# One graph and a list scheduler in place of hand-interleaved streams, with the spectral part reordered: block-sparse attention followed by a gated long convolution

## The chip, the cores and the metric

One core of a Trainium2 chip runs the whole kernel. The metric is device time in microseconds (us). The kernel before took 307.49 us (median of 3 runs, 306.24 to 308.87) when the prediction was made. Engine names are those of the profile: PE is TensorE (matmuls), PEld its weight loads, DVE is VectorE, ACT is ScalarE, POOL is GpSimd, SP the engine whose queue issues most DMAs.

## The reference

```python
# q, k, v: (4 batches, 8 heads, 768, 64) f32
k_rep = k.reshape(B, H, 12, 64, D).mean(axis=3)          # mean key of each block of 64
gate = einsum('bhsd,bhnd->bhsn', q, k_rep)               # causal; each query keeps its 3 best
                                                         # blocks and its own
attn = softmax(where(mask & causal, q @ k.T / 8, -1e9)) @ v
x = attn as (B, 768, 512)
x1, x2, x3 = split(x @ w_proj)                           # w_proj: 512 x 1536
x2c = irfft(rfft(x2, axis=1) * rfft(filter_fft, axis=0)) # circular convolution over 768
out = (x1 * x2c * x3) @ w_out
```

The DFT runs along the sequence and the projection along the features, so they commute: DFT(x) @ W2 = DFT(x @ W2). The change uses this.

## The kernel before

Work comes in 16 groups (a pair of heads in a batch). A group has a preparation (transposes of K and Q, the gate, the block mask), scores, exp, P@V and a normalisation. Four groups give a batch, on which the convolution part runs ("hyena" in the code). Scores are matmuls over 128 rows: 64 features, 12 rows that carry the block mask, 52 rows of zeros. All attention-phase results share 8 PSUM banks: 2 pairs for scores, 4 single ones for the rest.

Names in the lines below: `kn`, `qn`, `vn` are loaded K, Q and V; `kp`, `qp`, `xp` transposes; `kmb` (`km` after the change) the key sums of the blocks; `gn` the gate; `nm`, `mt`, `ms` the mask; `sp` the scores, `ex` their exp; `po` P@V; `xT` the transposed attention output, `xe` and `xo` (`eo` after) its even and odd sums; `x13p` and `prod` the projections x1 and x3 and their product; `Y` the filtered spectrum, `cv` its inverse transform, `yT` the gated product, `op` and `osb` the result. After the change every PSUM bank is called `ps`.

```python
    def score_piece(st, h, pi):                  # Kt, Qt: 128 rows, 76 of them used
        for (col, kc, q0, w) in PIECES[pi]:
            nc.tensor.matmul(sp[:, col:col + w], lhsT=kt[:, P * kc:P * (kc + 1)], rhs=qt[:, q0:q0 + w], ...)
        nc.scalar.activation(ex[:, 0:w], sp[:, 0:w], AF.Exp, scale=ESC)
    ...
    def pair_out(st, j):                         # per pair: transpose, even and odd sums
        ...
        nc.vector.tensor_copy(xT[:, j, :], xp[:, 0:S])
        eng.tensor_tensor(xe[:, j, :], xT[:, j, 0:HS], xT[:, j, HS:S], op=ALU.add)
        eng.tensor_tensor(xo[:, j, :], xT[:, j, 0:HS], xT[:, j, HS:S], op=ALU.subtract)
    ...
    def hyena_gen(st, last=False):               # per batch, after its four pairs
        for nm_, src in (("x2e", xe), ("x2o", xo)):
            for t in range(HC):
                for dc in range(DC):
                    nc.tensor.matmul(pp, lhsT=src[:, dc, P * t:P * (t + 1)], rhs=wp[:, dc, Dm:2 * Dm], ...)
                nc.scalar.copy(dst[:, t, :], pp)         # x2p -> x2e, x2o
                yield 0.85
        for c in range(HC):
            dft_fwd(x2[0], x2[1], c, 0, xa)              # then the DFT of the whole batch
            ...                                          # products t, spectrum Y, x13, cv, yT, op
```

The order comes from generators that each announce a guessed cost, merged by their progress; the framework's own scheduler may then still move instructions on all engines but SP.

```python
    def merge(streams):
        while True:
            live = [s_ for s_ in streams if s_.alive]
            if not live:
                return
            min(live, key=lambda s_: s_.key()).step()
    ...
            streams = [Stream(attn_gen(st), T_ATT), Stream(later_preps(b), NP * (T_PREP + 0.1))]
            ... streams.append(Stream(hyena_gen(prev), T_HY))      # the batch before
            merge(streams)
    ...
        with tc.manual_schedule(engines={mybir.EngineType.SP}):
            schedule()
```

The softmax here doesn't subtract the row's maximum and nothing guards it: scores larger than these inputs give would overflow.

## Time and profile before

| | before |
|---|---|
| median, us | 307.49 |
| span of the profiled run, us | 305.3 |
| PE / DVE / ACT / POOL busy, us | 254.0 / 218.7 / 176.3 / 138.0 |
| PE streaming (estimate, below), us | 216 |
| first score matmul (start), last P@V matmul (end), us from start | 18.0, 262.4 |

The page of the profiled run: busy time and share by engine, then the span in 40 equal slices (tenths busy), then the chain of work that ended last.

```profile
PE 254.0 (83%) x2309; PEld 153.9 (50%) x2309; DVE 218.7 (72%) x673; ACT 176.3 (58%) x277; POOL 138.0 (45%) x202
...
PE   3485897797999698987997798988996999899891
...
DMA  9998999699387308276759119094902000310005
...
PE 43%; DVE 31%; POOL 8%; ACT 6%; DMA 5%; issue 4%; SPq 1%; ACTq 0%; DVEq 0%
```

No engine is full, and the chain hops between PE and DVE. PE's busy time needs care: a 512-column matmul is logged with 0.38 us, but 24 of them in a row took 5.19 us in the traces, one per 0.216 us. In the same way I read 0.163 us at 384 columns (12 in 1.95 us) and 0.031 us for a P@V matmul of 65 (27 in 0.85 us). Counts times such spacings give the *PE streaming* used below, an estimate: 216 us for the whole program. (The Trainium skill, "Perfetto Trace Analysis", section "Identifying the Most-Contended Engine", says that matmul busy time is no good measure because matmuls are pipelined; the trace agrees: 254.0 us are logged where some 216 us stream.)

By stage: each row is a stretch of time, then its length, then busy us and instruction count of each engine, the granted clock, the DMA engines' share and GB/s.

```profile
core 0: us, PE busy (x) PEld busy (x) DVE busy (x) ACT busy (x) POOL busy (x), PEclk, DMA share, GB/s
0.00:79.00 79.00, 56.03 (x550) 36.96 (x551) 60.05 (x219) 52.00 (x75) 44.81 (x78) 0.98 0.97 184
79.00:145.00 66.00, 58.79 (x561) 35.91 (x560) 48.28 (x157) 37.38 (x62) 30.46 (x43) 0.95 0.55 115
145.00:211.00 66.00, 58.66 (x567) 35.91 (x565) 48.31 (x157) 39.94 (x65) 30.50 (x44) 0.97 0.57 123
211.00:262.00 51.00, 46.53 (x451) 28.55 (x449) 36.86 (x101) 31.51 (x49) 26.86 (x35) 0.97 0.24 52
262.00:305.30 43.30, 34.02 (x195) 16.57 (x191) 25.16 (x42) 15.49 (x30) 5.40 (x4) 0.98 0.19 73
```

### The profile page before, as it was taken

How to read it: one execution, taken by the hardware profiler on the slowest of the kernel's cores; microseconds unless marked ns; L12 is line 12 of the kernel's file. 1: busy time of each engine (PE TensorE's matmuls, PEld its weight loads, DVE VectorE, ACT ScalarE, POOL GpSimd, SP SyncE). 2: the span in 40 equal slices, each digit the busy share in tenths (PEclk: the TensorE clock that was granted, in tenths of full speed). 3: DMA queues.
4: the chain of work that ended last, by engine and by line, in shares of the span. 5: the costliest groups of instructions: out<-in, count | busy, mean ns of one | idle time of the engine just before them, and what ended most of it. 6: DMA issues, size and time to landing. Idle time of an engine off the chain costs nothing.

```text
span 305.3 us, 6432 instructions
## 1 busy us (share of the span) xinstructions
PE 254.0 (83%) x2309; PEld 153.9 (50%) x2309; DVE 218.7 (72%) x673; ACT 176.3 (58%) x277; POOL 138.0 (45%) x202
## 2 busy tenths in 40 slices
PE   3485897797999698987997798988996999899891
PEld 2332674464555366654654466544544566444430
DVE  7699985856589768665589768665599676339790
ACT  2349987584847435665856356656865467541314
POOL 7886226542339723532159453531188344205100
PEclk9999999997999789999999799999999899999999
DMA  9998999699387308276759119094902000310005
GB/s 169 215 261 198 140 210 179 144 173 201 72 152 139 73 1 164 50 150 201 179 104 184 29 34 178 5 268 151 196 19 50 4 6 3 139 67 2 0 0 206
DMA packets 87311, 36.00 MB, mean 118 GB/s; under 512 B 76936, under 2 KB 83440, under 8 KB 87280
## 3 DMA queue, kind: packets, MB, share of 16 engines
q1 hardware_dynamic: 85168, 33.50, 50.7%
q0 software_dynamic: 2112, 2.10, 4.7%
q8 instruction: 18, 0.29, 0.4%
q14 instruction: 13, 0.11, 0.1%
HBM read 24.64 MB, written 6.29 MB: 101 GB/s over the span
## 4 chain that ended last, share of the span: by engine, by line
PE 43%; DVE 31%; POOL 8%; ACT 6%; DMA 5%; issue 4%; SPq 1%; ACTq 0%; DVEq 0%
PE x13p L502 9%; PE sp L381 7%; PE x2p L462 6%; PE cv L519 4%; PE op L543 3%; PE po L400 3%; POOL Y L483 2%; DVE xe L424 2%; ACT ex L385 2%; PE gn L297 2%; DVE ks L268 2%; DMA Qt_104<-q2h 2%; PE qp L284 2%; PE kp L267 2%; DVE sd L526 2%
## 5 line engine op out<-in xcount | busy, mean ns | idle before, releaser
L385 ACT ACTIVATE ex<-sp 128x1024 f16<-128x1024 f32 (+1 forms) x96 | 86.9, 921 | 46.6 <-PE sp L381 42.9
L387 POOL TENSOR_SCALAR_AFFINE_SELECT ex<-ex 128x256 f16<-128x256 f16 x96 | 39.1, 413 | 105.4 <-ACT ex L385 104.8
L502 PE MATMUL x13p<-xT,wp 128*128 128x384 f16 x256 | 51.7, 337 | 4.9 <-DVE prod L510 1.4
L400 PEld LDWEIGHTS <-ex 128*128 128x128 f16 x672 | 33.4, 99 | 14.0 <-issue 2.3
L400 PE MATMUL po<-va,ex 128*128 128x65 f16 x672 | 38.4, 197 | 1.0 <-POOL ex L387 0.9
L502 PEld LDWEIGHTS <-wp 128*128 128x128 f16 x256 | 24.4, 99 | 21.0 <-issue 8.6
L543 PE MATMUL op<-wo,yT 128*128 128x512 f16 x96 | 24.5, 380 | 3.9 <-POOL yT L528 3.2
L528 POOL TENSOR_TENSOR yT<-prod,sd 128x768 f16<-128x768 f32 x12 | 21.7, 1810 | 5.1 <-DVE sd L527 5.1
L267 PE MATMUL kp<-id_91,kn 128*128 128x128 f32 x96 | 18.2, 308 | 4.8 <-DMA kn<-in_k_dram 4.8
L546 ACT COPY osb<-op 128x512 f32<-128x512 f32 x24 | 13.6, 589 | 14.6 <-PE op L543 12.3
L286 DVE SCALAR_TENSOR_TENSOR q2l<-qp,q2h 128x384 f16<-128x384 f32 x32 | 17.5, 553 | 6.0 <-ACT q2h L285 5.5
L284 PE MATMUL qp<-id_91,qn 128*128 128x128 f32 x96 | 18.7, 313 | 3.2 <-DVE xT L422 2.9
L268 DVE TENSOR_REDUCE ks<-kp 128x6 f32<-128x384 f32 x32 | 17.6, 551 | 4.7 <-PE kp L267 4.4
L519 PE MATMUL cv<-G,Y 128*128 128x384 f16 x96 | 20.9, 350 | 0.0
L285 ACT ACTIVATE q2h<-qp 128x384 f16<-128x384 f32 x32 | 15.7, 497 | 8.9 <-PE qp L284 8.2
L412 DVE TENSOR_TENSOR xn<-po,rec 128x384 f16<-128x384 f32 x32 | 17.8, 555 | 0.7
L250 POOL TENSOR_SCALAR_AFFINE_SELECT va<-vn 128x768 f16<-128x768 f32 x16 | 14.5, 903 | 5.5 <-DMA vn<-in_v_dram 5.4
L297 PEld LDWEIGHTS <-q2h 128*128 128x128 f16 x160 | 10.5, 101 | 12.3 <-issue 5.9
L284 PEld LDWEIGHTS qp<-id_91,qn 128*128 128x128 f32 x96 | 12.5, 160 | 7.7 <-DVE xT L422 4.1
L381 PE MATMUL sp<-Qt_104,Kt_98 128*128 128x512 f16 (+3 forms) x48 | 13.5, 373 | 2.8 <-DMA Qt_104<-q2h 1.4
L267 PEld LDWEIGHTS kp<-id_91,kn 128*128 128x128 f32 x96 | 11.8, 156 | 7.3 <-POOL rowv L128 4.7
L543 PEld LDWEIGHTS <-yT 128*128 128x128 f16 x96 | 8.1, 97 | 12.7 <-POOL yT L528 4.3
(318 smaller groups left out, 540.1 us busy)
## 6 DMA issues: line engine op xcount, KB each, us to landing
kn<-in_k_dram SPq DMA_DIRECT2D x32, 192.0 KB
qn<-in_q_dram SPq DMA_DIRECT2D x32, 192.0 KB
vn<-in_v_dram SPq DMA_DIRECT2D x16, 384.0 KB
out_dram<-osb SPq DMA_DIRECT2D x24, 256.0 KB
wp<-in_moe_w_proj_dram POOLq DMA_DIRECT2D x3, 512.0 KB, 6.4
Qt_104<-q2h SPq DMA_DIRECT2D x6, 96.0 KB
Qt_105<-q2h SPq DMA_DIRECT2D x6, 96.0 KB
Qt_106<-q2h SPq DMA_DIRECT2D x6, 96.0 KB
```

Source lines behind the costliest of these rows:

```text
L267: nc.tensor.transpose(kp[:, P * c:P * (c + 1)], kn[:, HC * hf + c, :, :], id32)
L268: nc.vector.reduce_sum(ks[:, 6 * hf:6 * hf + 6], kp[:, 0:HS].rearrange("p (n t) -> p n t", t=64), axis=AX.X)
L284: nc.tensor.transpose(qp[:, P * c:P * (c + 1)], qn[:, HC * hf + c, :, :], id32)
L381: nc.tensor.matmul(sp[:, col:col + w], lhsT=kt[:, P * kc:P * (kc + 1)], rhs=qt[:, q0:q0 + w], start=True, stop=True, skip_group_check=True)
L385: nc.scalar.activation(ex[:, 0:w], sp[:, 0:w], AF.Exp, scale=ESC)
L387: nc.gpsimd.affine_select(out=dv, in_=dv, compare_op=ALU.is_ge, fill=0.0, base=0, pattern=[[0, 2], [1, P]], channel_multiplier=-1)
L400: nc.tensor.matmul(po[:, 65 * c:65 * c + 65], lhsT=exs[pi][:, col:col + P], rhs=va[:, h % 2, kc, :], start=(kc == 0), stop=(kc == c), skip ...
L462: nc.tensor.matmul(pp, lhsT=src[:, dc, P * t:P * (t + 1)], rhs=wp[:, dc, Dm:2 * Dm], start=(dc == 0), stop=(dc == DC - 1))
L502: nc.tensor.matmul(xp[:, 0:HS], lhsT=wp[:, d2, base + P * dc:base + P * (dc + 1)], rhs=xT[:, d2, hs:hs + HS], start=(d2 == 0), stop=(d2 == ...
L519: nc.tensor.matmul(cv[:, 0:HS], lhsT=Y[:, 3 * par + n_, ds_], rhs=G[:, g_, :], start=(n_ == 0), stop=(n_ == 2))
L528: (nc.vector if last else nc.gpsimd).tensor_mul(yT[:, dc, :], prod, sd)
L543: nc.tensor.matmul(op, lhsT=yT[:, d2, P * c:P * (c + 1)], rhs=wo[:, d2, :], start=(d2 == 0), stop=(d2 == DC - 1))
```

## The change

The kernel is rewritten as 16 groups' and 4 batches' worth of operations in one graph, with modelled durations. A list scheduler inside the kernel picks at each step the operation that can start first; within 0.022 us of that, the one with the lowest stage key. It also picks the engine where two can do the work, and the buffer. The framework then keeps this order on all engines. With it come:

- the DFT runs per head pair, straight after that pair's attention, and the W2 projection after it;
- score matmuls contract over 76 rows, so the zero fills go;
- `km` goes from DVE to POOL; `xT`, even/odd sums, `ms`, `Y`, `yT` and some casts may go to either of two engines;
- deeper buffers (8 `ex` for 6, 8 `t` for 6, 3 K and Q for 2, ...);
- the first group's halves of K and Q are moved by DVE, not by DMA.

```diff
+PAR = dict(p0=-2.48, p1=-0.702, ..., h0=5.31, hlen=4.733, ..., pen_dve=0.414, ahead=3.869, delta=0.022, queue=1.557, direct=1)
+POOLS = dict(kn=3, qn=3, vn=2, ..., ex=8, rec=2, xn=2, eo=3, XT=7, xT=8, t=8, Y=1, x1=3, ..., osb=4)
 ...
-            nc.tensor.matmul(sp[:, col:col + w], lhsT=kt[:, P * kc:P * (kc + 1)],
+                        nc.tensor.matmul(o[:, col:col + w], lhsT=E.sb(Kt[g])[0:KR, t, P * kc:P * (kc + 1)],
 ...
+        for dst, op, f in ((E_, ALU.add, 0.0), (O_, ALU.subtract, 0.1)):      # from xn, per pair
+            add("eo", v(f), {"POOL": pol(0.87), "DVE": dve(HS, 2)}, e_eo, rd=xns, wr=[dst], lock=True)
+        ...                                                                   # st1: DFT of the pair
+            add("XT", v(.55 + .25 * p_), {"ACT": act(hi - lo), "DVE": dve(hi - lo)}, e_XT, rd=[st], wr=[(XT[g], p_)])
+                def e_s2(...):                                                # per batch: W2 on the spectrum
+                    nc.tensor.matmul(E.bk(xa), lhsT=w, rhs=E.wp[:, j, Dm:2 * Dm], ...)
 ...
+            m = min(c[0] for c in cands) + par["delta"]
+            est, o = min((c for c in cands if c[0] <= m), key=lambda c: (c[1].vt, c[1].i))
+            if best is None or est < best[0]:
+                best = (est, o, e)
 ...
-        with tc.manual_schedule(engines={mybir.EngineType.SP}):
-            schedule()
+    order = plan(PAR)
+    with tc.manual_schedule():
+        for o in order:
+            o.emit(E, nc, o.on)
```

## The prediction

> **What bounds the kernel now.** The page gives PE 254.0 us busy of a 305.3 us span (83%), DVE 218.7, ACT 176.3, POOL 138.0. PE busy overstates the array's work: in the timeline four 128x512 matmuls last 1.03 us together, 0.216 us apart, though each is logged as 0.38 us; 24 x13p matmuls took 4.06 us, 22 po matmuls 0.70. From such spacings I estimate 218 us of PE streaming, 71% of the span. (The Trainium skill, "Perfetto Trace Analysis", section on the most-contended engine, calls matmul busy a bad measure; this trace agrees.) No engine is saturated: the chain of waits is PE 43%, DVE 31%, POOL 8%, ACT 6%, DMA 5%. The loss is in-order queues waiting for each other.
>
> Stages: start to the first x2p at 79 us, with 38 us of PE streaming (waits for the first group's shuffles, 11.7 to 18.0, and for a V load, 39.7 to 45.7); two batch periods of 66 us with 53 us streaming each (81%); the last attention; a tail of 43 us after the last po at 262, 34 us streaming.
>
> **What the change does.**
> - PE work: unchanged. The DFT per pair streams about 0.99 us x16; before, 24 DFT matmuls per batch, half of them half-width pairs that start 0.01 us apart and so run together: 3.9 us per batch. Equal. W2 keeps 24 matmuls.
> - 76-row scores: no PE time, as streaming depends on columns; they save zero fills, about 11 us of POOL and 4 of DVE at the start.
> - DVE falls about 30 us to 188: kmb copies and subtracts (20 us) go to POOL, a third of xT, half of ms and some even/odd sums elsewhere; it takes more Y and yT.
> - ACT rises about 18 us to 195: x2p casts (14.1) go; XT evacuations (13), 11 xT (9) and 8 ms come. POOL near 130.
> - Order: each pair's DFT follows its attention, so the tail loses x2p-then-DFT; deeper buffers (8 ex, 8 xT, 8 t); the first group's shuffles by DVE, not DMA, about 5 us off the start.
>
> **On the critical path.** Almost all gain is idle PE removed, not work removed. First stage: ACT carries about 9.8 us of logged work per pair (ex 5.5), so five pairs plus 12 us of start give about 62 us until 40 us of PE work is done (79 before for 38). Middle: 141 us of streaming at 87% is 162. Tail: still 36 us of streaming after the last po (x13, cv, op in the order), at 90% is 40, plus 2 for the last store. Sum 265; with some overlap of stages 262.
>
> **Predicted: 262 us, 80% range 246 to 283.** Faster by over 2%: 0.94; within 2%: 0.04; slower: 0.02.
>
> **What would show it.** PE streaming still 218 us, now 83% of the span; logged PE busy within 5% of 254; DVE busy 175 to 200, ACT 185 to 205, POOL 120 to 145; first score matmul near 13 us (before 18); no 6 us DMA piece in the chain; last po to end 38 to 42 us; chain PE share above 50%, DVE below 25%. Row count wrong: 512-column score matmuls no longer 0.38 us.
>
> **What would make it wrong.** The order is frozen from modelled durations; where ACT or POOL runs longer than planned, in-order queues stall. Four single PSUM banks serve the attention phase as before; if these bind, the middle stays at 81% (about 275). DVE and POOL may slow one another: xe on DVE ranged 357 to 1603 ns. If plan and chip agree well, the middle reaches 93% and the time 248.

## More of the kernel before

The stages are: start and first batch's attention; two periods of attention of one batch with the convolution of the one before; the last attention; the last convolution alone. The matmul counts give PE streaming of 37.0, 52.5, 52.8, 42.0 and 31.9 us in them, so PE idles for 42.0, 13.5, 13.2, 9.0 and 11.4 us: 89 us in all.

Two cautions about this run. First, PE was granted only half its full clock (0.50 in the profile) in four stretches, 71.9 to 75.3, 102.6 to 109.4, 170.9 to 174.3 and 235.7 to 239.1 us, 17 us in all. There the 384-column matmuls came one per 0.320 us, not 0.163, and PE streamed only 8.7 us by the counts. So up to 8 of the 89 us are PE slowed and not PE waiting. Secondly, its 307.49 us is 1.8% above the fastest run of this kernel measured with it (302.08, later), so it is slow by the record's rule (over 1.5%).

What such idling looks like in the third stage, in order of time, first PE and then DVE (start, length, engine, line, operation; in brackets idle time before it and what ended it):

```profile
165.81 0.65 PE L502 MATMUL x13p<-xT,wp 128*128 128x384 f16 x3
167.47 0.55 PE L284 MATMUL qp<-id_91,qn 128*128 128x128 f32 x3 [1.00 <-DVE xT L422]
168.05 0.81 PE L502 MATMUL x13p<-xT,wp 128*128 128x384 f16 x4
170.41 0.20 PE L297 MATMUL gn<-kmb_112,q2h 128*128 128x24 f16 x2 [1.55 <-DVE prod L510]
```

```profile
165.50 1.32 DVE L276 TENSOR_TENSOR kmb_112<-ks,kmb_112 64x12 f16<-64x12 f32 x2
166.85 0.56 DVE L422 COPY xT<-xp 128x768 f16<-128x768 f16 x1
...
168.47 1.42 DVE L425 TENSOR_TENSOR xo<-xT 128x384 f16<-128x384 f16 x1
169.81 0.54 DVE L510 TENSOR_TENSOR prod<-x13p,x_2748 128x384 f32<-128x384 f32 x1
```

PE waits twice in 5 us for a PSUM bank that DVE has yet to empty, and DVE is late because a small `kmb` and an `xo` (1.42 us here; 0.35 us at best in this trace) stand ahead in its queue. These are the waits of in-order queues, not of a full engine.

## The result

| | before | after |
|---|---|---|
| median, us (4 runs each, the later measurement) | 306.87 (302.08 to 308.87) | 265.84 (264.44 to 267.15) |
| span of the profiled run, us | 305.3 | 264.6 |
| PE / DVE / ACT / POOL busy, us | 254.0 / 218.7 / 176.3 / 138.0 | 240.4 / 190.9 / 183.6 / 137.9 |
| PE streaming, us | 216 (71%) | 216 (82%) |
| first score (start), last P@V (end), us | 18.0, 262.4 | 24.0, 224.7 |

The ratio is 0.876 (95% interval 0.8655 to 0.8865). Ratios are the mean time of one kernel's runs over that of the other's of the same rounds, so not quite the ratio of the medians quoted. Executions over 1.5% slower than the fastest of the same kernel are left out of the means. By the ratio the gain is about 38 us (265.84 / 0.876 is 303.5); the two profiled runs are 41 us apart, as the one of before is a slow one.

The same lines of the page after:

```profile
PE 240.4 (91%) x2400; PEld 159.9 (60%) x2400; DVE 190.9 (72%) x612; ACT 183.6 (69%) x302; POOL 137.9 (52%) x246
...
PE   0778979789799979999999999999999999999994
...
DMA  8988579969899999799858661120233000014106
...
PE 70%; DVE 12%; DMA 6%; ACT 4%; issue 3%; POOL 3%; SPq 1%; DVEq 0%; ACTq 0%; POOLq 0%
```

The slices show two regimes: up to about the sixteenth slice (110 us) PE has gaps and the DMA engines are near full; from there PE reads 9 throughout, save in the last slice. The stretches, with a row for each regime and one for what follows the last P@V:

```profile
core 0: us, PE busy (x), PEclk, DMA share, GB/s
0.00:110.00 110.00, 89.55 (x945) 0.98 0.93 184
110.00:224.70 114.70, 114.60 (x1253) 1.00 0.44 107
224.70:264.60 39.90, 36.24 (x211) 0.99 0.22 80
```

By the matmul counts PE streams 69 of 110, then 112 of 114.7, then 35 of 39.9 us. Its idle time is 41 + 2 + 5 = 48 us, against 89 before: the 41 us between the two profiles. Up to 6 of them may be the granted clock and not the order, as this run had 3.4 us at half clock before its end (49.0 to 52.4, with 1.4 us of streaming) and the one of before 17.0 (with 8.7). Most of the gain is not the clock's: on the second chip below, a run of the kernel before at a mean clock of 0.993 took 300.56 us, 33 us above the changed kernel beside it (267.59 us at 0.981 to 0.987).

The stretches above are not the stages of before. At equal work (an estimate from the same counts) the changed kernel reaches the ends of those five stages at 72, 131, 185, 228 and 265 us. It needs 72, 59, 54, 43 and 36 us for what took 79, 66, 66, 51 and 43, so 7, 7, 12, 8 and 7 us are won, about two thirds of it in the three middle stages. The list of what PE waited for between 110 and 265 us is empty. A piece of the middle, to set beside the piece of before:

```profile
131.38 0.49 PE L341 MATMUL ps<-id,qn 128*128 128x128 f32 x3
131.71 0.35 PE L485 MATMUL ps<-va,ex 128*128 128x65 f16 x6
131.89 0.60 PE L457 MATMUL ps<-qt,kt 76*128 76x512 f16 x3
132.33 0.45 PE L485 MATMUL ps<-va,ex 128*128 128x65 f16 x9
132.62 0.65 PE L714 MATMUL ps<-G,Y 128*128 128x384 f16 x3
```

Each line starts before the one above has ended and none has a bracket with a wait: preparation, P@V, scores and convolution of different groups alternate in batches of 3 to 9 matmuls.

PE streaming done by a given time (us; matmul counts of the trace, times spacings), the measure on which the experiments are compared:

| time, us | before | after | framework order | DFT per batch | engines nailed | 128 rows, first try | few loads |
|---|---|---|---|---|---|---|---|
| 30 | 7 | 9 | 5 | 9 | 10 | 4 | 9 |
| 70 | 33 | 36 | 30 | 32 | 32 | 32 | 38 |
| 110 | 60 | 69 | 59 | 62 | 63 | 63 | 73 |
| 150 | 94 | 107 | 93 | 100 | 100 | 100 | 112 |
| 190 | 125 | 146 | 130 | 138 | 137 | 139 | 150 |
| 230 | 158 | 186 | 168 | 176 | 176 | 178 | 190 |

Here too the half clock counts as lost streaming. Before 110 us it was granted for 3.4 us in the changed kernel and in the one with the framework's order, 10.2 with few loads and with engines nailed, 13.6 with the DFT per batch, 6.8 with 128 rows; after 110 us in none of these six, save at the very end.

### The profile page after: what moved, and what is told of

It reads as the page before. It is cut to its first block, busy times and chain, and to the rows that moved or that the text cites. A ratio compares the mean times of both kernels' runs of the same rounds, so it can differ in the third digit from the quotient of the medians.

```text
span 264.6 us, 6689 instructions
## 1 busy us (share of the span) xinstructions
PE 240.4 (91%) x2400; PEld 159.9 (60%) x2400; DVE 190.9 (72%) x612; ACT 183.6 (69%) x302; POOL 137.9 (52%) x246
## 4 chain that ended last, share of the span: by engine, by line
PE 70%; DVE 12%; DMA 6%; ACT 4%; issue 3%; POOL 3%; SPq 1%; DVEq 0%; ACTq 0%; POOLq 0%
PE ps L687 14%; PE ps L457 11%; PE ps L745 8%; PE ps L485 7%; PE ps L714 6%; PE ps L651 6%; DMA kn<-in_k_dram 4%; PE ps L309 4%; PE ps L341 3%; PE ps L542 3%; DMA vn<-in_v_dram 2%; PE ps L417 2%; PE ps L376 2%; PE ps L549 2%; DVE t L660 2%
## 5 line engine op out<-in xcount | busy, mean ns | idle before, releaser
L463 ACT ACTIVATE ex<-ps 128x1024 f16<-128x1024 f32 (+1 forms) x96 | 86.8, 924 | 12.8 <-PE ps L457 10.9
L457 PE MATMUL ps<-qt,kt 76*128 76x512 f16 (+3 forms) x256 | 53.7, 315 | 1.1 <-ACT ex L463 1.1
L687 PE MATMUL ps<-xT,wp 128*128 128x384 f16 x256 | 51.5, 325 | 0.1
L485 PE MATMUL ps<-va,ex 128*128 128x65 f16 x672 | 36.3, 195 | 2.9 <-POOL ex L468 2.1
L670 POOL TENSOR_TENSOR Y<-t,t 128x512 f16<-128x512 f32 (+1 forms) x21 | 27.3, 1303 | 15.6 <-DVE t L660 14.9
L457 PEld LDWEIGHTS <-kt 76*128 76x128 f16 x256 | 22.9, 100 | 16.4 <-issue 3.1
L651 PE MATMUL ps<-wp,XT 128*128 128x512 f16 x96 | 24.6, 379 | 0.0
L735 POOL TENSOR_TENSOR yT<-prod,sd 128x384 f16<-128x384 f32 x17 | 18.1, 1068 | 11.5 <-DVE sd L729 10.0
L745 PE MATMUL ps<-wo,yT 128*128 128x512 f16 x96 | 23.8, 379 | 0.0
L341 PE MATMUL ps<-id,qn 128*128 128x128 f32 x96 | 18.7, 309 | 2.8 <-DVE xn L498 1.3
L714 PE MATMUL ps<-G,Y 128*128 128x384 f16 x96 | 20.8, 326 | 0.0
```

Source lines behind the costliest of these rows:

```text
L341: nc.tensor.transpose(E.bk(qp)[:, P * c:P * (c + 1)], E.sb(qn[g])[:, HC * hf + c, :, :], E.id32)
L457: nc.tensor.matmul(o[:, col:col + w], lhsT=E.sb(Kt[g])[0:KR, t, P * kc:P * (kc + 1)], rhs=E.sb(Qt[g])[0:KR, t, q0:q0 + w], start=True, sto ...
L463: nc.scalar.activation(E.sb(ex)[:, 0:w], E.sp(sp)[:, 0:w], AF.Exp, scale=ESC)
L485: nc.tensor.matmul(o[:, 65 * c:65 * c + 65], lhsT=E.sb(exs[pi])[:, col:col + P], rhs=E.sb(va[g])[:, t, kc, :], start=(kc == 0), stop=(kc = ...
L651: nc.tensor.matmul(E.bk(xa), lhsT=w, rhs=E.wp[:, j, Dm:2 * Dm], start=(j == 0), stop=(j == NP - 1))
L670: (nc.vector if en == "DVE" else nc.gpsimd).tensor_tensor(E.sb(Y)[ro, n_, :], E.sb(x)[ri, :], E.sb(y)[ri, :], op=op)
```

## The experiments

Theory: the work is the same, and the gain is PE idle time removed by the order, mostly in the middle. Rivals: the gain comes from one of the parts that came along (DFT per pair, balance of engines, deeper buffers, 76 rows, direct move). All runs were correct unless said otherwise. Three groups ran on three chips. On the second chip five of the seven runs of the kernel before were slow (300.56 to 310.56 us in all), and its kernels are compared with the changed kernel run beside them. For the others "+x us" is the difference of the ratio from 0.876, times 306.9 us; each ratio's interval is about 0.008 to either side, and that of 0.876 is 0.0105, so differences under 4 us are not clear.

### The framework's order (label fworder)

```diff
-    with tc.manual_schedule():
+    with tc.manual_schedule(engines={mybir.EngineType.SP}):
```

> The changed kernel's graph, engines, buffers and issue order, but the framework's scheduler may reorder PE, DVE, ACT and POOL again, as it did in the kernel before. Main theory (the gain is the order, which keeps PE fed): 275 to 295 us, and PE waits come back after 110 us, where the changed kernel has none. Rival (restructured graph, deeper buffers and balance are enough, any sane order serves): 262 to 270 us.

Measured: 284.51 us, ratio 0.9364 (0.9311 to 0.9417), +18.5 us. Same operations, engines and buffers. Matmuls and busy times by stretch:

```profile
0.00:30.00 30.00, 12.02 (x65) 7.12 (x65) 17.56 (x65) 12.74 (x24) 12.46 (x27) 1.00 1.14 200
30.00:110.00 80.00, 69.04 (x727) 46.94 (x728) 49.22 (x188) 55.46 (x87) 41.57 (x83) 0.98 0.68 149
110.00:260.00 150.00, 145.61 (x1505) 97.53 (x1505) 114.92 (x341) 105.64 (x174) 77.10 (x132) 1.00 0.42 102
```

The first score comes at 33.3 us and not 24.0. Out of the chain of waits of that start:

```profile
17.22 3.65 SPq L260
20.91 7.70 DMA kn<-in_k_dram
28.75 0.89 PE ps L309 x3
29.73 0.56 DVE ks L312
```

In DVE's queue the sums `ks` of a later K, which lands only at 28.6 us, stand ahead of the first group's mask `nm`: its maxima are done at 27.6 us, it begins at 30.2. PE is 10 us of streaming behind by 110 us; it loses another 8 by 230 us, where PE waits again: of 3.7 us listed between 110 and 260 us, 1.8 are for the mask `nm` and 0.8 for `xT`. So the order alone carries about half of the gain, and more of it before 110 us than the theory said.

### A wider window for equal starts (label keyorder1)

```diff
-    ... delta=0.022, ...
+    ... delta=1.0, ...
```

> The changed kernel, with the list scheduler's window for equal starts widened from 0.022 to 1.0 us: it then takes the operation with the lowest stage key among those ready within 1 us, even if another could start sooner. All work, buffers and tables are the same. Main theory: 280 to 300 us, more PE waits in the middle. Rival (order hardly matters): 262 to 270 us.

Measured: 280.05 us (2 runs, one round; verdict unclear), ratio 0.922, about +14 us. The same graph, ordered a little less by "what can start first", loses over a third of the gain. It points the way of the run above but is not the order alone: the scheduler also chose engines anew (POOL busy 124.4 us, not 137.9; DVE 196.8, not 190.9), and this profile had 10.2 us at half clock.

### The DFT per batch again (label batchdft)

```diff
-        for p_ in range(2):                       # st1: DFT of the pair
-            ...
+        for i in range(2):                        # x2p: W2 on the batch's even and odd sums, casts on ACT
+            for t in range(HC): ...
+        for c in range(HC):                       # then the DFT of the batch
+            for kind in range(2): ...
```

> The changed kernel with the spectral part as before: W2 projection on the even and odd sums of the whole batch, casts on ACT, then the DFT per batch; all else (list scheduler, engines, other buffers) kept, stage keys not tuned for it. Main theory (order, not the DFT per pair, gives the gain): 266 to 280 us, so at least two thirds of the 41 us stay. Rival (the DFT per pair gives the gain): 290 us or more.

Measured: 277.12 us, ratio 0.9146 (0.9064 to 0.9228), +11.8 us. About seven tenths of the gain stay, as the theory had it, but the part is no trifle. PE streaming in all is the same (216.0 against 216.3 us), yet it is 7 us behind at 110 us and then keeps that distance to 150 us and about 9 to 230 us. Before the first convolution can start, the pair's DFT is work for PE that depends on nothing but that pair. Without it PE has more gaps: from 30 to 110 us its listed waits are 13.3 us, against 8.0 in the changed kernel. One of them:

```profile
58.10 1.03 PE L457 MATMUL ps<-qt,kt 76*128 76x512 f16 x6
60.28 0.57 PE L341 MATMUL ps<-id,qn 128*128 128x128 f32 x3 [1.15 <-DMA qn<-in_q_dram]
```

That the missing DFT opens these gaps is argued, not shown: the stage keys were tuned for the other graph, and up to 5 of the 7 us by 110 us may be this profile's half clock (13.6 us, with 6.8 of streaming). The time itself is not the clock's: a run at 0.992 took 277.37 us.

### Engines nailed as before (label fixeng)

```diff
-        add("km", v(.3), {"POOL": pol(0.6)}, ...)
+        add("km", v(.3), {"DVE": (1.0, 1.15)}, ...)
-            add("eo", v(f), {"POOL": pol(0.87), "DVE": dve(HS, 2)}, ...)
+            add("eo", v(f), {"DVE": dve(HS, 2)}, ...)
         # xT, ms, G: DVE; XT, x1, ce, osb: ACT; Y, yT: POOL, in the last batch partly DVE
```

> The changed kernel, but each operation that the scheduler may place on one of two engines is nailed to the engine of the kernel before: km copies, xT, even and odd sums, ms and G on DVE; casts on ACT; Y and yT on POOL until the last batch. DVE busy should rise by 20 to 30 us to 210 to 220. Main theory (order is most, the balance of engines some): 270 to 285 us. Rival (balance is the main gain): 285 us or more. Second rival (DVE has slack, balance is worth nothing): within 1% of the control.

Measured: 278.83 us against 267.59 us of the control (after2), +11.2 us. DVE busy rises to 204.0 us only, 13 us above the changed kernel, below the 20 to 30 us expected, which had left out that nailing Y and yT to POOL takes work off DVE (L670 and L735 on DVE: 19.6 us in the changed kernel, 7.7 here). All 32 even/odd sums are on DVE here; the kernel before had 6 of them on POOL. ACT falls to 171.6 us, POOL to 124.3. Before 110 us PE is 6 us behind, at 230 us 10. So the balance counts although no engine but PE is ever full. The Trainium skill ("Perfetto Trace Analysis", section "Optimizing Scalar/DVE Operations") warns that work moved from DVE to GpSimd might not help, as they share an SBUF read port. In these traces the sharing is visible: in the kernel before, the 12 even/odd sums on DVE with no POOL instruction beside them took 346 to 359 ns, the 14 with one took 550 to 1603. The placement helped all the same; which moves did is not separated.

### The control (label after2) and the buffers (label buf)

```diff
-POOLS = dict(kn=3, qn=3, ..., ex=8, ..., eo=3, ..., t=8, ..., x1=3, ..., osb=4)
+POOLS = dict(kn=2, qn=2, ..., ex=6, ..., eo=2, ..., t=6, ..., x1=2, ..., osb=3)
```

> The changed kernel itself again, as the control of this group. Every theory: 0.866 of the kernel before, give or take 0.01; 262 to 268 us.

> The changed kernel with the buffer counts of the kernel before where both have the buffer: 2 K, 2 Q, 6 ex, 6 t, 2 x1, 3 osb, and 2 even/odd pairs; the plan is made again for them. Main theory: within 2% of the control (262 to 271), as no waits for these buffers lead the list. Rival (the deeper buffers let the engines run ahead and give the gain): 280 us or more.

Measured: 267.59 us for the control and 265.16 us with fewer buffers, one per cent less. The deeper buffers give nothing that shows here. (The pools for `xT`, XT, `va` and the like were left.)

### 128 rows, first try (label rows128)

```diff
-                        nc.tensor.matmul(..., lhsT=E.sb(Kt[g])[0:KR, ...], rhs=E.sb(Qt[g])[0:KR, ...])
+                        nc.tensor.matmul(..., lhsT=E.sb(Kt[g])[0:P, ...], rhs=E.sb(Qt[g])[0:P, ...])
-            nc.vector.memset(E.t["qt"][i][64:KR, :, 0:P], 0.0)
+            nc.gpsimd.memset(E.t["qt"][i][64:P, :, :], 0.0)
+            nc.gpsimd.memset(E.t["kt"][i][64:P, :, :], 0.0)
```

> The changed kernel, but its score matmuls contract over all 128 rows again, with zero fills of the spare rows on POOL at the start. If the row count is worth nothing (main theory), the 512-column score matmuls still log 0.39 us and the time stays within 1% of the changed kernel's 265.8 us. Rival (fewer rows make the array faster or raise the granted clock): at least 5 us slower than 265.8, with a lower clock than 0.99 or longer score matmuls.

Measured: 275.81 us, ratio 0.9072 (0.8994 to 0.9149), +9.6 us: a miss. Yet the matmuls are no slower. The score group after and in this run (count, busy us, mean ns), then what PE waited for most:

```profile
L457 PE MATMUL ps<-qt,kt 76*128 76x512 f16 x96 | 37.6, 393 | 1.1 <-ACT ex L463 1.1
```

```profile
L458 PE MATMUL ps<-qt,kt 128*128 128x512 f16 x96 | 36.8, 385 | 1.1 <-ACT ex L464 0.7 <-DMA qt<-ms 0.3
```

```profile
PE ps L218 <- DVE colv L174: 16.1, 1, 16.1
```

393 ns at 76 rows, 385 at 128. (The Trainium skill, "TensorE: Matmul & The Clock Gate", section "Step-by-step: what each phase is for", says that weight loads depend on the columns and not on the rows; 100 and 99 ns here agree.) What is lost is at the start: eight fills of 1.4 to 1.8 us stand in POOL's queue, DVE's mask copies wait for them, a one-element write of the sine table's input (L174) stands behind those copies, and PE gets its first matmul at 16.1 us, not 6.7. The first score comes at 33.2 us. All that follows is 7 us late to the end.

### 128 rows, fills out of the way (label rows128b)

```diff
+                if i < 1:        # first buffer pair: by ACT, idle then
+                    nc.scalar.activation(E.t[x_][i][64:P, :, :], <a zero, broadcast>, AF.Copy, ...)
+    # the other three: POOL, after the first three V casts; their mask rows copied later
```

> 128 rows in the score matmuls again, as in the first such run, but with the zero fills put where they delay little: the first buffer pair is cleared by ACT, which idles then, the others by POOL later. That first run lost 10 us and its first score came at 33 us, not 24. If the loss is the fills' place at the start (theory), first score near 24 us again and a time within 1.5% of the control, 263 to 271 us. If the array itself is slower with 128 rows (rival), 273 us or more.

Measured: 267.92 us, ratio 0.8757 (0.8688 to 0.8827), equal to the changed kernel; the first score comes at 25.8 us. So the row count itself is worth nothing that shows here (the intervals leave some 4 us), and the fills cost where they stand.

### The first group's halves by DMA (label shufdma)

```diff
-    ... direct=1,
+    ... direct=0,
```

> The changed kernel with the first group's K and Q halves and its mask moved by DMA, as in the kernel before, not by DVE and ACT; the plan is made again. The prediction gave the direct move 5 us. If so: first score 4 to 7 us later than 24 us and 270 to 274 us in all. Rival (the start waits for DVE, not for these moves): within 1% of the control.

Measured: 270.40 us, ratio 0.8844 (0.8765 to 0.8923), +2.6 us, inside the intervals. The first score moves to 29.3 us, 5.3 us later. This does not show that the direct move of the halves is worth 5 us. The last thing the first score waits for here is the mask by DMA (27.21 to 29.27 us), and the kernel before had moved that mask by DVE (L337, at 13.9 us), against what was expected above. Besides, all four runs had a low clock (0.935 to 0.949), at half from 22.4 to 46.3 us in the profile. The share of each is open; at the end all of it together costs 2.6 us, which is not clear of noise.

### Few loads (label noload)

```diff
-                    nc.sync.dma_start(E.sb(dst)[:, :, t, :], ...)
+                    nc.sync.dma_start(E.sb(dst)[0:np_, :, t, :], ...)     # np_ = 128, from the fourth group on 2
```

> Wrong result on purpose: the changed kernel with the same order, but the K, Q and V loads from the fourth group on bring only 2 of 128 partitions, so that most of the DMA work is gone. If DMA limits the stretch from 30 to 110 us, in which PE streams only 47 of 80 us (theory), PE fills up there and the time falls by 8 to 20 us, to 246 to 258. If ACT and the in-order queues limit it (rival), less than 3 us is gained.

The result is wrong. Measured: 261.94 us against 267.59 of the control, -5.7 us: less than the range of the theory, more than the rival allowed. The second rows of both, control first:

```profile
30.00:110.00 80.00, 70.97 (x820) 49.62 (x819) 54.23 (x203) 58.12 (x92) 48.83 (x94) 0.96 0.96 187
```

```profile
30.00:110.00 80.00, 72.72 (x875) 51.04 (x874) 56.45 (x216) 60.53 (x97) 49.84 (x96) 0.98 0.40 81
```

The DMA share falls from 0.96 to 0.40, but only some 4 us of PE streaming is gained by 110 us. Loads explain about 5 of the 20 us that PE idles between 30 and 110 us. In the control 6.8 us of that stretch were at half clock (3.6 us of streaming), so up to 3 more are the clock's. The rest is open; waits there are spread over many short ones.

### Mending the start (labels start3 and best)

```diff
     order = plan(PAR)
+    move(<mask rows on POOL>, behind the index rows)
+    <the four buffers' mask fills on DVE>: behind the first group's q2l and the first three masks
```

> The changed kernel with its plan kept, but at the start POOL makes the index rows before the mask rows, and DVE fills the four K and Q buffers' mask rows later, not ahead of the table work. If DVE's queue at the start holds the first score at 24 us (theory), the first table matmul moves from 6.7 to about 5 us, the first score to 19 to 22 us, and the time falls by 2 to 5 us. If not (rival), within 1 us.

> The same mending of the start together with the smaller buffer counts, which had cost nothing (265.2 us against 267.6 of the control). Theory: the two are independent, so 260 to 264 us, the fastest correct kernel. Rival: the same as the control.

Measured: 266.95 us for the first (one of its four runs was slow), ratio 0.8703 (0.8616 to 0.8790), and 268.47 us, ratio 0.8766 (0.8690 to 0.8842), together with the smaller buffers. Neither is clearly different from the changed kernel: a miss. The first table matmul did move, from 6.7 to 3.6 us, but the first score stayed at 24.7. The chain of the start in the first of these runs:

```profile
2.47 4.87 DMA kn<-in_k_dram
7.34 0.14 issue
7.47 0.89 PE ps L309 x3
...
13.09 1.25 DVE prod L225 x2
...
17.58 1.00 DVE ks L312 x2
```

The chain had begun with DVE's fills; now it begins with the load of K, which lands at 7.3 us, while the next three table matmuls stand behind the K transposes in PE's queue. After that the table work (`prod`) and the moved fills still pass through DVE ahead of the first mask. No version here beats the changed kernel by a clear margin.

## Why the prediction was right, and where it was not

- **The time.** 262 predicted, 265.84 measured, inside 246 to 283. The mechanism held: PE streaming stayed at 216 us and rose from 71% to 82% of the span (218 us and 83% predicted), the chain's PE share went to 70% and DVE's to 12%. The experiments show that no one part is the whole cause: undone singly, the order costs 18.5 us, the DFT per pair 11.8, the engine choice 11.2, and the rest within noise when well placed. They overlap; the sum is not to be read as a budget.
- **The middle, term of the sum too long.** The prediction took 141 us of streaming at 87%, 162 us. Measured: the 40th us of streaming was done at 75 us, the last P@V at 224.7, so 150 us, or 94%. This is the prediction's own best case for the middle (93%), which it had put at 248 us in all; the start kept the time from it.
- **The first stage, term too short.** 62 us were predicted until 40 us of PE work; it took 75. The step that failed is "first score matmul near 13 us (before 18)": it came at 24.0. From there to the 40th us of streaming it is 51 us, close to the 50 that the sum gave to five pairs, so the mis-sized term is its "12 us of start", measured as 24. Why: the new order puts the sine table ahead of the first exp (L233 from 10.5 to 16.1 us; before, from 23.8 us on, after the first score), and that work, with the mask fills, stands in DVE's and ACT's queues from 1 to 20 us. This is read from the timeline; the run that moved the fills left the first score at 24.7, and none took the sine table out of the start. These two errors, +13 and -12 us, nearly cancel by luck: the terms as measured, 75, 150 and 40 us, add up to the 265 of the prediction's sum. The total was better than its parts.
- **The tail.** 38 to 42 us predicted from the last P@V to the end; 39.9 measured, with 35 us of streaming (36 predicted). Though the projection and the DFT no longer stand one after the other there, the tail's PE work is not less than before (32 us); the gain is that PE idles less in it (5 us, not 11).
- **"No 6 us DMA piece in the chain" was wrong.** A V load of 5.94 us and K loads of 5.13 and 5.28 us are in the chain after. Attention runs earlier, so the same bytes are wanted in less time (argued); taking most of them away gave 5.7 us (noload).
- **Busy times.** DVE 190.9 (175 to 200 predicted) and POOL 137.9 (120 to 145) are as said. ACT at 183.6 is just under 185 to 205: the prediction missed that sorting the sines ahead of the exps leaves 3 table loads for 7, at 1.28 us each 5.1 us less, about half of the 11 us by which ACT is under its 195. Logged PE busy of 240.4 is just outside "within 5% of 254".
- **The 76 rows.** "No PE time" is shown (393 and 385 ns; rows128b). That the fills matter at the start was right in kind; the first try showed that badly placed they cost 9.6 us.
- **The four single PSUM banks** did not bind in the middle: PE waited for nothing from 110 us on.

## What to carry to other kernels

When no engine is full and the chain of waits hops between engines, add up what the busiest one really needs (spacing in a run of instructions, not logged length) before you remove work: here 38 us lay in order, placement and dependency, save what the clock did, and none in the amount of PE work. Once an engine is full for the rest of the kernel, what it loses earlier is carried to the end: fills badly placed at the start cost 9.6 us for a first score 9.2 us later, while mending one input of the first score gave nothing, because another was just as late. With the static order PE waited for nothing from 110 us on; what is left to gain here lies in the first 110 us (41 us idle), of which loads explain about 5 and the rest is not settled. And look at the granted clock of a profile before you call a gap a wait.

## What the Trainium skill lacked or had wrong

- "TensorE: Matmul & The Clock Gate", section "Back-to-back issue gap", gives about 131 ns per matmul as the sustained figure at 512 columns with weight loads. Here 24 such pairs in a row took 5.19 us, 0.216 us each, which is its isolated figure; the measurement decides.
- "ScalarE: Activation LUTs", section "What ACT_TABLE_LOAD costs", counts about 2.66 us for a switch, load and drain. Here the load took 1.28 us (24.79 to 26.07), the work before it had ended at 24.77 and the exp began at 26.08: no further 1.38 us is seen.
- "Perfetto Trace Analysis", section "Identifying the Most-Contended Engine", takes LDWEIGHTS busy time, beside the share of peak FLOPs, as a measure of headroom. From 110 to 224.7 us, where PE waited for nothing and streamed 112 us, PEld was busy 79.49 of 114.7 us, 69%: by itself it does not show that PE is full.
- No page warns that a static order can put set-up work of a side product (here, as read from the timeline, the sine tables) ahead of the first main work: first score at 24.0 us after, 18.0 before.
